# Batch 0 of a banded attention in 32 by 64 blocks, with a new order for the opening of the kernel

## The chip, the cores and the metric

One NeuronCore of a Trainium2 chip runs the whole kernel. The metric is device time in microseconds (us), the median of three runs: 878.97 us for the kernel before (878.5 to 879.45). The engines are TensorE (PE: matmul; PEld: its weight loads), VectorE (DVE), ScalarE (ACT), GpSimd (POOL) and SyncE (SP, which here only issues DMAs).

## The reference, cut to what matters

```python
# q, k, v: (8 batches, 8 heads, 576 positions, 64)
scores = q @ k.T / sqrt(64)                      # per batch and head
rel = pos[:, None] - pos[None, :]
mask_plain = (rel >= 0) & (rel < 32)                              # heads 0 to 3
mask_dil = (rel >= 0) & (rel < 128) & (rel % 4 == 0)              # heads 4 to 7
scores = where(mask, scores, -1e9); scores -= scores.max(-1)
attn = exp(scores); attn /= attn.sum(-1) + 1e-9
x = (attn @ v), heads side by side               # 4608 tokens x 512
h = x @ w_in                                     # 512 -> 2048
g = where(h >= 1, h, where(h <= -1, 0, (h + 1)**2 / 4))
return g @ w_out                                 # 2048 -> 512
```

The dilated heads become plain bands when positions are sorted by their remainder modulo 4, so every 32 queries need at most 64 keys.

## The kernel before, in words

The second half, two matrix products over 4608 tokens, is nearly all of the work. Tokens go in 9 tiles of 512; a *step* is one tile and one 128-wide slice of the 2048 hidden values: 144 steps, of which step s has tile s // 16 and slice f = s % 16. Each product is made of three fp32r products (high by high, low by high, high by low), so `layer1` (L788) of a step is 4 chunks of 3 matmuls of 128x512 and `layer2` (L861) is 4 blocks of 3. Between them stand, on ScalarE and VectorE, y = clamp(h) (L798), its square (L801), h = max(h, y) (L804), the high part of g (L815) and its low part (L819).

The weights arrive as pairs of 32-bit words and are made into high and low parts during the first 16 steps, one `wi` and one `wo` for each slice. For one of them: `scaled` (ScalarE, L218), `low_bits` (ScalarE, L224), `joined` (VectorE, L228), `high_part` (ScalarE or GpSimd, L236) and `low_part` (GpSimd, L240).

The attention of two heads (a *pair*, named by its first head n: 0, 2, 4, 6 are batch 0, 8 to 14 are batch 1) gives one of the four 128-wide chunks of x. Batch 1 is computed in blocks of 32 queries by 64 keys: 72 score matmuls for a pair (L319), ten masked minima on VectorE (L347), `exp` on ScalarE, a guard and a reciprocal, a product with the reciprocal (L407), five transposes (L434), copies to SBUF (L443), 72 value matmuls (L483), and the high and low part of x (L518, L523). Batch 0 has another path: blocks of 64 queries by 96 keys (`scores_block`, L330; minima L290), which leaves the last 64 queries of every head over; these form the *tail*, which has its own scores, softmax, transposes and values (`tail_*`, L535 to L618) between steps 2 and 4. Softmax of a pair is either *by tiles* (ScalarE subtracts the minimum and sums while it takes exp, one instruction for each tile) or *whole* (GpSimd subtracts, L373; ScalarE takes exp in one instruction, L364; VectorE sums, L377).

All that happens before step 18 is recorded from a table, `OPENING`. Each engine executes its instructions in the order in which the table's tokens stand; an engine never overtakes. A token names an operation and what it works on: `S8` scores of pair 8, `r8.3` minimum of tile 3, `z8` subtraction, `e8` exp, `u8` sum, `i8` guard, `R8` reciprocal, `n8` product with it, `T8.0` transposes, `p8.0` copy, `V8` values, `x8...` and `l8...` high and low part of x, `A2.1` chunk 1 of layer 1 of step 2, `y2 s2 j2 g2 d2` the five operations between the layers, `B2.3` block 3 of layer 2, `awi4 bwi4 jwi4 hwi4 lwi4` the five steps of a weight, `wi4`, `q8`, `k8`, `v8` loads (all on SP's queue), `W3` three filler matmuls (`spin`), `tS` to `tl` the tail. From step 18 on, the rest (`burst`, L767, and `plan`) follows fixed rules that the change does not touch; the first burst is in step 18 and needs the PSUM banks that batch 1 used. `PLACES` says which PSUM bank a tile of the opening takes. Until they are needed for weights, the places of late weights hold batch 0's inputs (`home`).

```python
        PE.matmul(out=bank[:, :128], lhsT=half, rhs=half, start=True, stop=True)
        for token in OPENING.split():
            play(token)
```

Of the kernel before, what the change touches and what calls it, by code (L numbers as in the profile page):

```python
# [25 lines left out]
F32 = mybir.dt.float32  # L26
# [8 lines left out]
WIN, DIL = 32, 4  # L35
QT, NQ = 96, 6
# [7 lines left out]
BQ, BK, NB = 64, 96, 8  # L44
TAIL = NB * BQ
# [10 lines left out]
T5 awi1 tS0 i7 R7 l0 jwi1 q8 wi3 k8 n7 tS2 tS4 tS6 x2 p5 p4 hwi1 bwi2 lwi0 T7 V4 awo0 bwo0 lwi1 wo2 wo1 l2 tr5 tr0 p7
tr6 tr2 tr1 tr4 V6 A0.0 awi2 x4 wi4 x6 A0.1 tr7 tr3 jwo0 l4 tz A0.2 te l6 jwi2 hwo0 A0.3 A1.0 A1.1 A1.2 A1.3 S8 tu
awi3 bwi3 hwi2 y0 jwi3 s0 ti j0 g0 lwo0 lwi2 hwi3 S10 d0 r8.1 tR r8.5 r8.4 r8.9 A2.0 A2.1 A2.2 bwo1 awo1 r10.1 r10.4
y1 r10.2 r8.0 r8.2 r8.7 r10.6 r8.3 r8.6 r8.8 wo5 v8 tv wo3 q14 wi6 k14 wi7 wi5 wo10 wo9 wi9 wi8 lwi3 z8 s1 awi4 r10.7
j1 A2.3 B0.3 B0.0 B0.1 g1 d1 r10.0 jwo1 tn hwo1 lwo1 A3.0 A3.1 A3.2 tT bwo2 e8 awo2 bwi4 tp A3.3 B1.1 tV u8 y2 jwi4  # L60
wo4 s2 i8 hwi4 tx R8 r10.5 j2 n8 lwi4 y3 tl r10.3 r10.8 r10.9 bwo3 g2 bwi6 awi5 B1.0 B1.3 B0.2 B1.2 d2 jwo2 awi6 s3
bwi5 jwi5 hwo2 z10 A4.0 A4.1 A4.2 A4.3 T8.0 T8.1 lwo2 e10 p8.0 awo3 p8.1 hwi5 B2.1 B2.0 B2.2 B2.3 V8 j3 lwi5 wi10 wo8
wo11 wo7 wi13 v10 wi11 wo6 k12 bwi7 g3 bwo4 x8.1.0 jwo3 y4 d3 u10 jwi6 A5.0 A5.1 i10 hwo3 x8.0.0 x8.1.1 R10 l8.1.0
l8.0.0 lwo3 hwi6 A5.2 B3.3 A5.3 B3.0 B3.2 awo4 q12 wi12 bwi9 s4 jwo4 l8.1.1 j4 n10 hwo4 B3.1 T10.0 T10.1 g4 bwi10
p10.0 lwi6 lwo4 d4 y5 awi7 awi8 p10.1 s5 bwi8 bwo5 awo5 A6.0 B4.3 B4.2 B4.1 A6.1 A6.2 A6.3 B4.0 V10 jwi7 j5 jwi8 jwo5
# [1054 lines left out]
```

## Time and profile before

| | |
|---|---|
| median of 3 runs | 878.97 us |
| profiled execution | 878.36 us, of which the span shown in the trace is 876.5 us |
| PE busy | 866.6 us, 99% of the span |
| DVE, ACT, POOL busy | 578.2 us (66%), 368.9 us (42%), 144.8 us (17%) |
| chain that ended last | PE 94% of the span |
| granted clock of TensorE | 0.999 of full speed |

The time outside the span (1.86 us) is start and end of the execution. A busy share of 99% says that hardly any time is left in which PE has nothing to do; it does not say that all it does is useful, since the filler matmuls at the beginning count as busy too. So the profile is read for two things: when the first matmul of layer 1 can start, and what PE does or waits for after that.

### The profile page before, as it was taken

The page shows a single profiled execution, that of the slowest core. Times are in us where ns is not written, and L with a number is a line of the kernel's source. Part 1 is how long each engine was busy: PE and PEld are TensorE (multiplying, and loading weights), DVE is VectorE, ACT ScalarE, POOL GpSimd, SP SyncE. Part 2 cuts the span into 40 slices and gives each one's busy share as a digit, 9 for nine tenths or more (in the row PEclk, how much of TensorE's full clock was granted, in tenths as well). Part 3 has the DMA queues.
Part 4 walks back from the last instruction along what each step waited for, and adds up shares of the span by engine and source line. Part 5 has one row for each costly group of instructions (what it writes and reads, how often), then busy time and mean ns, then how long its engine had stood idle before and what let it go on. Part 6 is the DMA issues. An engine that isn't in the chain of part 4 may idle for free.

```text
span 876.5 us, 19402 instructions
## 1 busy us (share of the span) xinstructions
PE 866.6 (99%) x7903; PEld 713.8 (81%) x7903; DVE 578.2 (66%) x1538; ACT 368.9 (42%) x969; POOL 144.8 (17%) x147
## 2 busy tenths in 40 slices
PE   8999999999999999999999999999999999999998
PEld 7777887888888888888888888888888888888886
DVE  5866746878777777777777777777777543334333
ACT  6788744443533444344443443334434222222222
POOL 4767630111111111111110011111111000000000
PEclk9999999999999999999999999999999999999999
DMA  9993302231221112111211131101200010001001
GB/s 345 373 371 116 94 28 76 61 106 57 86 72 31 34 54 101 55 56 56 104 56 55 56 105 57 42 28 61 87 28 29 1 49 1 0 1 49 1 0 49
DMA packets 25434, 66.45 MB, mean 76 GB/s; under 512 B 2816, under 2 KB 4096, under 8 KB 25344
## 3 DMA queue, kind: packets, MB, share of 16 engines
q1 hardware_dynamic: 25056, 64.97, 21.3%
q8 instruction: 62, 1.02, 0.5%
q14 instruction: 28, 0.23, 0.1%
q10 hardware_dynamic: 288, 0.23, 0.1%
HBM read 55.75 MB, written 9.44 MB: 74 GB/s over the span
## 4 chain that ended last, share of the span: by engine, by line
PE 94%; DVE 2%; ACT 1%; DMA 1%; POOL 1%; issue 1%; DVEq 0%; SPq 0%; POOLq 0%; ACTq 0%
PE h L788 44%; PE acc L861 44%; PE att L767 4%; PE spare L767 1%; DMA wi_raw<-w_in 1%; PE o L483 0%; PE s L319 0%; DMA tc_place<-block_in 0%; DVE thirds L228 0%; ACT c_place L367 0%; POOL wo L240 0%; POOL wi L240 0%; DVE xf L712 0%; ACT gh L815 0%; PE t L434 0%
## 5 line engine op out<-in xcount | busy, mean ns | idle before, releaser
L861 PE MATMUL acc<-wo,gh 128*128 128x512 f32 x1134 | 375.2, 390 | 0.1
L788 PE MATMUL h<-xh,wi 128*128 128x512 f32 x1152 | 359.0, 393 | 0.0
L788 PEld LDWEIGHTS h<-xh,wi 128*128 128x128 f32 x1152 | 213.9, 188 | 45.5 <-DVE gl L819 0.3
L861 PEld LDWEIGHTS acc<-wo,gh 128*128 128x128 f32 x1134 | 212.8, 188 | 45.0 <-POOL wo L240 0.8
L801 ACT ACTIVATE y<-y,consts 128x512 f32<-128x512 f32 x144 | 104.2, 724 | 290.4 <-DVE y L798 290.3
L788 PE MATMUL h<-xl,wi 128*128 128x512 f32 x576 | 224.8, 390 | 0.1
L861 PE MATMUL acc<-wo,gl 128*128 128x512 f32 x567 | 221.1, 390 | 0.0
L819 DVE TENSOR_TENSOR gl<-h,gh 128x512 fp32r<-128x512 f32 x142 | 98.2, 692 | 86.4 <-ACT gh L815 85.7
L798 DVE TENSOR_SCALAR y<-h 128x512 f32<-128x512 f32 x144 | 99.4, 690 | 74.6 <-PE h L788 72.9
L804 DVE TENSOR_TENSOR h<-h,y 128x512 f32<-128x512 f32 x144 | 100.7, 699 | 67.7 <-ACT y L801 66.6
L815 ACT CAST gh<-h 128x512 fp32r<-128x512 f32 x142 | 83.3, 587 | 129.2 <-PE acc L861 79.2
L788 PEld LDWEIGHTS h<-xl,wi 128*128 128x128 f32 x576 | 108.2, 188 | 23.8 <-POOL xl L733 1.1
L861 PEld LDWEIGHTS acc<-wo,gl 128*128 128x128 f32 x567 | 106.5, 188 | 22.4 <-DVE gl L819 0.3
L696 POOL TENSOR_TENSOR c<-c 128x576 f32<-128x576 f32 x24 | 27.7, 1154 | 439.5 <-DVE c L693 439.5
L712 DVE STREAM_TRANSPOSE xf<-att 32x320 f32<-32x320 f32 x192 | 91.8, 478 | 3.9
L680 ACT ACTIVATE c<-c 128x64 f32<-128x64 f32 x216 | 72.5, 338 | 50.8 <-DVE c L667 50.8
L700 DVE STREAM_TRANSPOSE pt<-c 32x288 f32<-32x288 f32 x192 | 89.9, 468 | 3.2
L733 POOL TENSOR_TENSOR xl<-xf,xh 128x384 fp32r<-128x384 f32 (+7 forms) x48 | 41.5, 876 | 63.6 <-ACT xh L729 63.4
L680 ACT ACTIVATION_READ_ACCUMULATOR c<-c 128x1 f32 x216 | 40.7, 188 | 0.0
L667 DVE CUSTOM_DVE_ANT_0 c<-att,near 128x64 f32<-128x64 f32 x144 | 22.8, 220 | 24.6 <-PE att L767 24.6
L729 ACT CAST xh<-xf 128x384 fp32r<-128x384 f32 (+7 forms) x48 | 25.1, 575 | 1.8 <-DVE xf L712 1.8
L240 POOL TENSOR_TENSOR wo<-thirds,wo 128x512 fp32r<-128x512 f32 x16 | 22.4, 1400 | 13.8 <-ACT wo L236 13.3
(127 smaller groups left out, 453.6 us busy)
## 6 DMA issues: line engine op xcount, KB each, us to landing
thirds<-near_v_in SPq DMA_DIRECT2D x24, 576.0 KB, 4.1
out<-out SPq DMA_DIRECT2D x35, 256.0 KB, 2.8
kr<-k_in SPq DMA_DIRECT2D x28, 304.0 KB, 4.8
wi_raw<-w_in SPq DMA_DIRECT2D x16, 512.0 KB, 7.7
wo_raw<-w_in SPq DMA_DIRECT2D x16, 512.0 KB, 8.7
qr<-q_in SPq DMA_DIRECT2D x28, 288.0 KB, 5.0
vt<-v_in SPq DMA_DIRECT2D x8, 288.0 KB, 6.0
v_place<-vb_in SPq DMA_DIRECT2D x4, 512.0 KB, 8.9
```

The lines of the kernel that those rows point to most:

```text
L680: nc.scalar.activation(out=c, in_=c, func=AF.Exp, bias=self.st[:, 0, tile : tile + 1], scale=-1.0, accum_out=self.st[:, 1, tile : tile + 1],)
L700: nc.vector.transpose(out=self.pt[r : r + 32, TILES * (g // 2) : TILES * (g // 2 + 1)], in_=self.c[32 * g : 32 * g + 32, :, 32 * half : 32 ...
L712: nc.vector.transpose(out=x[r : r + 32, g % 2, :, :count], in_=values[:, :, :, 32 * half : 32 * half + 32])
L733: nc.gpsimd.tensor_tensor(out=xl, in0=x, in1=xh.bitcast(F32), op=ALU.subtract)
L767: PE.matmul(out=o, lhsT=a, rhs=b, start=True, stop=True)
L788: PE.matmul(out=hps[s], lhsT=ready[f"wi{f}"][:, w, 128 * c : 128 * c + 128], rhs=x[:, c], start=c == 0 and i == 0, stop=c == NC - 1 and i ...
L798: nc.vector.tensor_scalar(out=y, in0=hps[s], scalar1=-1.0, scalar2=1.0, op0=ALU.max, op1=ALU.min)
L801: nc.scalar.activation(out=ys[s], in_=ys[s], func=AF.Square, bias=half_t, scale=0.5)
L804: nc.vector.tensor_tensor(out=hps[s], in0=hps[s], in1=ys.pop(s), op=ALU.max)
L815: nc.scalar.copy(out=gs[s][0], in_=hps[s])
L819: nc.vector.tensor_tensor(out=gl, in0=hps.pop(s), in1=gh.bitcast(F32), op=ALU.subtract)
L861: PE.matmul(out=acc[m], lhsT=g[:, r], rhs=w[:, part], start=f == 0 and i == 0, stop=(f == NF - 1 or s == len(steps) - 2 and m == TOK // 12 ...
```

## The change

Batch 0 goes through the code of batch 1. `scores_block`, `reduce`, the tail and their inputs (`qb`, `kb`, `vb`, `vbt`, `block_in`) are gone; `q_in`, `k_in` and `v_in` now hold batch 0 too. `OPENING`, `PLACES` and `home` are new tables. Some operations may be VectorE's that were ScalarE's: `low_bits` of four weights, the guard of pairs 0 and 2, more of the copies after transposes, one high part of x. Pair 6 is normalised by VectorE as pair 4 was; other weights are cast by GpSimd. In batch 0, pair 0 is whole and pairs 2 and 6 by tiles, pair 4 whole; in batch 1, all four pairs are by tiles, where they were whole.

```diff
-BQ, BK, NB = 64, 96, 8
-TAIL = NB * BQ
...
 OPENING = """
-k2 q2 W7 k0 q0 msk Q0 K0 W6 q4 k4 wi0 k6 q6 mk1 S2.0 S0.0 S2.1 S0.1 v0 v2 wi1 v6 wi2 mk2 S0.2 S0.3 S2.3 S2.2 r0.3 r0.1
...
+W7 k0 q0 q2 mk3 k2 q4 k4 k6 q6 wi0 mk2 W2 S0 v0 wi1 wo0 v2 r0.6 r0.2 r0.4 r0.7 r0.8 r0.9 r0.5 r0.0 r0.3 r0.1 S2 S4 S6
...
-    thirds = pool.tile([128, 3 * DM], U32, tag="m", name="thirds")
-    near_vt = thirds.bitcast(F32)[:, : BLOCKS * D].rearrange("p (n m d) -> p n m d", n=2, d=D)
...
-    cast_by_pool = ('wi0', 'wo0', 'wi3', 'wo1', 'wo2', 'wi6', 'wi8', 'wo8', 'wi12', 'wi13', 'wi15', 'wi14', 'wo13', 'wo15')
+    cast_by_pool = ('wi0', 'wo0', 'wi2', 'wi3', 'wo1', 'wo2', 'wo3', 'wi8', 'wo6', 'wi12', 'wi15', 'wo13', 'wo14', 'wo15')
...
-        m = floats[w] = thirds[:, DM * (third % 3) : DM * (third % 3 + 1)]
+        m = floats[w] = third_pool.tile([128, DM], U32, tag=f"m{third % 3}", name=f"m_{w}")
...
+    low_by_vector = ('wi5', 'wo15', 'wo12', 'wi15')
+
     def low_bits(w):
+        if w in low_by_vector:
+            low = words(w)[0]
+            nc.vector.tensor_scalar(out=low, in0=low, scalar1=29, scalar2=None, op0=ALU.logical_shift_right)
+            return
...
-    kept_by_vector = {1, (12, 0), 3, 7}
+    kept_by_vector = {(0, 0), (2, 0), (2, 1), (4, 0), (6, 0), (6, 1), (8, 0), (10, 0), (12, 0), (14, 0), (14, 1)}
...
+    x_by_vector = {(10, 1, 1)}
...
-    copied_by_vector = (2,)
+    copied_by_vector = (2, 3)
...
         elif token == "mk3":
-            nc.sync.dma_start(out=near, in_=near_in.rearrange("p (k j) -> p k j", k=6))
+            nc.scalar.dma_start(out=near, in_=near_in.rearrange("p (k j) -> p k j", k=6))
...
+    value_pool = ctx.enter_context(tc.tile_pool(name="value", bufs=1))
+    near_vt = value_pool.tile([128, 2, BLOCKS // 2, D], F32, name="near_vt")
```

How the order moves, on three engines. First PE around the end of layer 1 of step 1 before: `h_1` is the PSUM tile of step 1, `s_0` and `s_1` the score banks of pair 8, a matmul of 128x512 is layer 1, one of 32x64 a score block.

```order
L788 MATMUL h_1_505<-xh_366,wi_420 128x512 x2
L788 MATMUL h_1_505<-xl_367,wi_420 128x512
L319 MATMUL s_0_519<-kr_404,qr_400 32x64 x2
L319 MATMUL s_1_520<-kr_404,qr_400 32x64 x4
L319 MATMUL s_0_519<-kr_404,qr_400 32x64 x4
```

And the same place in the changed kernel: `acc_0` is the output tile of layer 2, `h_2` the tile of step 2.

```order
L574 MATMUL h_1_646<-xh_439,wi_581 128x512 x2
L574 MATMUL h_1_646<-xl_440,wi_581 128x512
L650 MATMUL acc_0_689<-wo_639,gh_683 128x512
L650 MATMUL acc_0_689<-wo_639,gl_684 128x512
L650 MATMUL acc_0_689<-wo_639,gh_683 128x512
L574 MATMUL h_2_693<-xh_439,wi_641 128x512 x2
L574 MATMUL h_2_693<-xl_440,wi_641 128x512
```

Before, the scores of pairs 8 and 10 stand behind step 1 and then step 2 follows; now a block of layer 2 of step 0 stands there at once, and the scores of pairs 8 and 10 come later, among steps 3, 0 and 1.

VectorE of the changed kernel ahead of the first low parts of x that pairs 4 and 6 give: `m_wi`, `m_wo` are weights in the making (`joined`), `xl` a low part of x, `pts` the copy of transposes, `c_place` a pair's softmax.

```order
L320 TENSOR_TENSOR c_place<-c_place,stats 128x576
L190 SCALAR_TENSOR_TENSOR m_wi_459<-m_wi_459,wi_raw 128x512
L404 TENSOR_TENSOR xl_440<-o_0_468,xh_439 128x288
L340 COPY pts_xl<-t_0_532 128x512
L340 COPY pts_xl<-t_1_537 128x128
L404 TENSOR_TENSOR xl_440<-o_1_469,xh_439 128x224
L190 SCALAR_TENSOR_TENSOR m_wo_579<-m_wo_579,wo_raw 128x512
L190 SCALAR_TENSOR_TENSOR m_wi_585<-m_wi_585,wi_raw 128x512
L404 TENSOR_TENSOR xl_440<-o_0_539,xh_439 128x2x128
L404 TENSOR_TENSOR xl_440<-o_1_540,xh_439 128x2x128
```

The stretch that stood there before, between the low part of pair 0 and that of pair 4 (L523 is the low part, L550 the tail's minima; each minimum has a second row, for its result):

```order
L523 TENSOR_TENSOR xl_367<-o_346,xh_366 128x512
L550 ISA tc_place<-tsb,tc_place 64x96
L550 ISA tc_place 64x1
L550 ISA tc_place<-tsa,tc_place 64x96
L550 ISA tc_place 64x1
L439 COPY pts_xl<-t_424 96x512
```

Eight minima of the tail have gone from VectorE's list there; the normalisation of pair 6, copies and smaller low parts have come.

ScalarE ahead of the high part of weight wi4, before (`wi_750` in the first fence, `wi_898` in the second): `c_518` and `c_729` are the softmax of pair 8.

```order
L364 ACTIVATE c_518<-c_518 128x576
L218 ACTIVATE thirds<-wo_raw 128x512
L224 ACTIVATE wi_raw<-wi_raw 128x512
L588 COPY pt_68<-tt 96x512
L801 ACTIVATE y_743<-y_743,consts 128x512
L392 ACTIVATE stats<-stats 128x9
L236 CAST wi_750<-thirds 128x512
```

and now:

```order
L587 ACTIVATE y_769<-y_769,consts 128x512
L399 CAST xh_445<-o_1_591 128x2x16
L174 ACTIVATE m_wi_776<-wi_raw 128x512
L186 ACTIVATE wi_raw<-wi_raw 128x512
L284 ACTIVATE c_729,stats<-c_729,stats 128x64 x9
L308 ACTIVATE stats<-stats 128x9
L198 CAST wi_898<-m_wi_717 128x512
```

One exp of 128x576 has become nine of 128x64, each with a sum, and they stand right ahead of the cast of wi4.

## Rows read from the trace of the kernel before

**Rows 1.** Waits of PE from 26 to 150 us: total, times, longest.

```profile
PE att L767 <- DVE xl L523: 1.1, 1, 1.1
```

**Rows 2.** Timeline of PE: start us, us, line, tiles, count, idle before and releaser.

```profile
0.92 5.17 PE L265 MATMUL h<-consts 128*128 128x128 f32 x26 [0.92 <-DVE consts L979]
...
12.95 0.61 PE L429 MATMUL t<-tc_place,c 128*96 128x128 f32 x4 [1.11 <-DMA tc_place<-block_in]
...
15.30 1.28 PE L265 MATMUL h<-consts 128*128 128x128 f32 x10
...
26.28 0.73 PE L788 MATMUL h<-xh,wi 128*128 128x512 f32 x2
...
28.46 0.63 PE L788 MATMUL h<-xh,wi 128*128 128x512 f32 x2
...
31.99 1.73 PE L319 MATMUL s<-kr,qr 64*32 64x64 f32 x144
33.66 0.73 PE L788 MATMUL h<-xh,wi 128*128 128x512 f32 x2
...
40.60 0.60 PE L584 MATMUL tt<-tc_place 128*96 128x128 f32 x4
...
42.52 0.45 PE L598 MATMUL to<-pt,tv_place 96*64 96x64 f32 x8
...
43.39 0.50 PE L861 MATMUL acc<-wo,gh 128*128 128x512 f32 x1
...
46.26 0.62 PE L788 MATMUL h<-xh,wi 128*128 128x512 f32 x2
...
48.99 0.71 PE L434 MATMUL t<-ident,c 128*128 128x128 f32 x5
...
52.49 1.25 PE L483 MATMUL o<-pt,vt 64*64 64x32 f32 x72
```

**Rows 3.** The load issued second (1.1 to 1.2 us): size, us to landing.

```profile
q_place<-qb_in SPq DMA_DIRECT2D x1, 288.0 KB, 3.6
```

**Rows 4.** Timeline of DVE, columns as in rows 2.

```profile
7.29 0.26 DVE L290 CUSTOM_DVE_ANT_0 c<-s,tc_place 128x96 f32<-128x96 f32 x1 [6.42 <-PE s L330]
...
19.22 0.55 DVE L407 TENSOR_TENSOR c_place<-c_place,sums 128x384 f32<-128x384 f32 x1
...
22.17 1.22 DVE L228 SCALAR_TENSOR_TENSOR thirds<-thirds,wi_raw 128x512 uint32<-128x512 uint32 x1
...
26.55 0.69 DVE L228 SCALAR_TENSOR_TENSOR thirds<-thirds,wo_raw 128x512 uint32<-128x512 uint32 x1
...
32.37 0.69 DVE L819 TENSOR_TENSOR gl<-h,gh 128x512 fp32r<-128x512 f32 x1 [0.65 <-ACT gh L815]
...
35.21 0.22 DVE L347 CUSTOM_DVE_ANT_0 c<-s,near 128x64 f32<-128x64 f32 x1
...
35.35 0.22 DVE L347 CUSTOM_DVE_ANT_0 c<-s,near 128x64 f32<-128x64 f32 x1
...
38.77 0.74 DVE L377 TENSOR_REDUCE stats<-c 128x9 f32<-128x576 f32 x1
```

**Rows 5.** Timeline of POOL, columns as in rows 2.

```profile
22.80 2.97 POOL L240 TENSOR_TENSOR wi<-thirds,wi 128x512 fp32r<-128x512 f32 x2
...
36.15 1.15 POOL L373 TENSOR_TENSOR c<-c,stats 128x576 f32<-128x576 f32 x1 [2.21 <-DVE stats L347]
...
42.86 0.29 POOL L406 TENSOR_TENSOR c<-c,stats 128x64 f32<-128x64 f32 x1 [1.91 <-DVE stats L398]
43.23 1.15 POOL L407 TENSOR_TENSOR c<-c,stats 128x576 f32<-128x576 f32 x1
44.34 1.29 POOL L240 TENSOR_TENSOR wi<-thirds,wi 128x512 fp32r<-128x512 f32 x1
```

**Rows 6.** Timeline of ACT, columns as in rows 2.

```profile
37.85 0.67 ACT L364 ACTIVATE c<-c 128x576 f32<-128x576 f32 x1
...
156.54 0.33 ACT L680 ACTIVATE c<-c 128x64 f32<-128x64 f32 x1
```

More of the change, by code (lines that the diff above doesn't have):

```diff
@@ L56 @@
[L56 to L65, printed above, removed]
@@ new lines @@
+x4.0.0 x4.1.0 l2.1.0 jwo0 jwi2 l4.0.0 l4.1.0 x6.1.0 bwi3 x6.0.0 lwi1 hwo0 hwi2 A0.1 A1.0 A0.2 lwo0 lwi2 awi3 l6.1.0
+l6.0.0 A0.3 A1.1 A1.2 y0 A1.3 jwi3 x6.0.1 x4.0.1 bwo1 x4.1.1 s0 hwi3 j0 lwi3 g0 y1 d0 B0.0 A2.0 s1 awo1 A2.1 A2.2
+l6.0.1 l4.0.1 l2.1.1 j1 jwo1 A2.3 g1 awi4 hwo1 d1 A3.0 A3.1 S8 lwo1 y2 awo2 bwo2 s2 x6.1.1 awi5 bwi4 wi6 wo3 v8 wo8
+wo6 wi7 wi9 k12 wo7 wo10 wo15 wo4 wo5 wi8 wo9 jwo2 r8.8 l6.1.1 r8.5 r8.1 r8.9 r8.6 r8.0 r8.7 r8.3 r8.2 j2 r8.4 B1.0
+A3.2 B0.1 B1.1 S10 B0.3 A3.3 B1.3 e8.7 e8.0 e8.2 e8.8 e8.5 e8.3 e8.4 e8.6 e8.1 jwi4 bwi5 i8 hwi4 g2 r10.9 r10.6 r10.0
@@ L319, in scores @@
             PE.matmul(out=out, lhsT=q0, rhs=k0, start=True, stop=True)
-    def scores_block(n, t):
-        if n not in scored:
-            for j in range(2):
-                scored[n + j] = bank(f"s{n + j}")
-        for half in range(2):
-            first = 2 * BQ * t + BQ * half if n < H // 2 else (CLS + 32) * t + BQ * half
-            for j in range(2):
-                r = slice(64 * j, 64 * j + 64)
-                PE.matmul(
-                    out=scored[n + j][BQ * half : BQ * (half + 1), BK * t : BK * (t + 1)],
-                    lhsT=whole["q", n][r, BQ * (2 * t + half) : BQ * (2 * t + half + 1)],
-                    rhs=whole["k", n][r, first : first + BK],
-                    start=True,
-                    stop=True,
-                )
     def lowest(n, t):
-        if n < H:
-            kind = 0 if t == 0 or n >= H // 2 else 1
-            return reduce(n, t, (scored[n][:, BK * t : BK * (t + 1)], bmsk()[:, kind]))
         j, slot = divmod(t, 4) if t < 8 else (t - 8, 4)
@@ L492, in pieces @@
         if h < H // 2:
-            first = part * 3 * QT
-            cuts = sorted({first, min(max(end, first), first + 3 * QT), first + 3 * QT})
+            first = part * HALF
+            cuts = sorted({first, min(max(end, first), first + HALF), first + HALF})
             for a, z in zip(cuts, cuts[1:]):
@@ L509, in pieces, with x_high @@
         return out
[L511 to L521 removed]
+    x_by_vector = {(10, 1, 1)}
+    def x_high(n, part, piece):
+        src, t, place = pieces(n, part)[piece]
+        copy = nc.vector.tensor_copy if (n, part, piece) in x_by_vector else nc.scalar.copy
+        copy(out=place(xtile(t)[0][:, n % H // 2]), in_=src)
@@ L522, in x_low @@
+    def x_low(n, part, piece):
+        src, t, place = pieces(n, part)[piece]
         xh, xl = (x[:, n % H // 2] for x in xtile(t))
         nc.vector.tensor_tensor(out=place(xl), in0=src, in1=place(xh).bitcast(F32), op=ALU.subtract)
-    def tail_scores(n):
-        if "s" not in tail:
-            tail["s"] = [bank("tsa"), bank("tsb")]
-        at = BK * (n // 2)
-        for j in range(2):
-            r = slice(64 * j, 64 * j + 64)
-            q0, k0 = whole["q", n][r, TAIL:], whole["k", n][r]
-            o = tail["s"][j][:, at : at + BK]
-            if n < H // 2:
-                PE.matmul(out=o[r], lhsT=q0, rhs=k0[:, TAIL : TAIL + BK], start=True, stop=True)
-                continue
-            k0 = k0.rearrange("p (c i) -> p c i", c=DIL)[:, :, 128:]
-            for w in range(2):
-                PE.matmul(
-                    out=o[64 * j + 32 * w : 64 * j + 32 * w + 32].rearrange("p (c i) -> p c i", c=2),
-                    lhsT=q0[:, 32 * w : 32 * w + 32],
-                    rhs=k0[:, 2 * w : 2 * w + 2],
-                    start=True,
-                    stop=True,
-                )
@@ L1067 @@
-    vbt = np.stack(vbt, axis=1).reshape(BK, 12 * D)
-    row, col = np.arange(128)[:, None], np.arange(BK)[None, :]
-    at = row % BQ
-    normal = (col > at) & (col <= at + WIN)
-    begins = normal & ((row >= BQ) | (col >= 32))
-    last = (col // 48 == at // 16 % 2) & (col % 48 > at % 16) & (col % 48 <= at % 16 + WIN)
-    block = [np.where(m, 0.0, NEG).astype(np.float32) for m in (begins, normal, last)]
-    block = np.concatenate([*block, np.eye(128, dtype=np.float32)], axis=1)
-    def filled(a):
-        return np.concatenate([a, np.zeros((128 - a.shape[0], a.shape[1]), a.dtype)])
```

332 lines of the change are left out of this document (74 added, 258 removed), and 10 rows, old and new, of the table PLACES.

## The prediction

> **What bounds the kernel now.** I read three views in this order: the waits of PE, PE's timeline over the opening, and then the timelines of the engines that feed it there. The waits show that once layer 1 of step 0 has begun, PE stands still once: 1.1 us before the first burst in step 18, for a low part of x [rows 1]. So the span of 876.5 us is 26.28 us until that beginning, and a stream of matmuls behind it with almost no hole [rows 2]. Three things can change the time: when the stream starts, how much PE work stands in it, and what waits are in it. That other engines are busier or idler counts only where it moves one of these. The opening is a chain through all engines: PE runs fillers until the scores, VectorE takes minima from 7.29 us on [rows 4], and the first transposes wait 1.1 us for the identity's load [rows 2]. The profiled execution took 878.36 us, 0.61 below the median of 878.97; I work in differences and take them off the median.
>
> I compare the two kernels at one point, the first matmul of step 2. Before it is at 33.66 us [rows 2].
>
> **The start of the scores.** Nine fillers stand ahead instead of 13. The 13 took 5.17 us as 26 matmuls, 0.40 each [rows 2], so nine end at 4.5. Now k0 and q0 are loaded first. The second load landed 3.6 us after its issue at about 1.16, so at 4.8 [rows 3]; the mask beside it is twice as large, so I take 5.0. One pair's scores are half of 1.73 [rows 2], with the pipeline's filling 1.0, so VectorE can begin at 6.1 instead of 7.29 [rows 4].
>
> **From the minima to the values.** A minimum of 128x64 follows the one before it in 0.14 to 0.15 [rows 4], so ten end at 7.6. Pair 0 is done whole: subtraction 1.15 on GpSimd [rows 5] to 8.9, exp 0.67 on ScalarE [rows 6] behind two tiles of pair 2, to 9.6, sum 0.74 on VectorE [rows 4] behind other minima to 10.4, guard and reciprocal to 10.8, product 0.29 and 1.15 on GpSimd [rows 5] to 12.4. The identity is now behind 192 + 4 x (304 + 288) + 512 KB of loads, 3.1 MB with itself, as before with its smaller pieces; it let the transposes start at 12.95 [rows 2], and I take 12.8. So the first transposes gain almost nothing: the 1.2 us of the earlier start go into a softmax that is half as wide again on GpSimd and VectorE.
>
> Then PE's list is bound by what it holds: transposes of pair 2 behind GpSimd's next product at 14.1, values of pair 0 (1.25 to 1.3, [rows 2]) to 15.8, eight fillers of 0.256 (1.28 for five, [rows 2]) to 17.9. Pair 4's transposes wait for its product on VectorE: 0.55 for 384 columns [rows 4] makes 0.83 for 576, with 0.25 for the extra tile, behind a `joined` and a sum, so 18.7. Pair 2's values then run to 20.5, where layer 1 of step 0 begins, against 26.28. But its chunk 0 needs pair 0 alone; transposes of pair 6 (0.5), two value products (1.3 each) and three chunks (0.69 each) follow, and chunk 3 could start at 25.8 by PE.
>
> VectorE has more to do until then. From the product of pair 4 it still has three low parts, a copy of 0.6, pair 6's product (1.1), two more copies, three `joined`, two low parts of pair 2 and four of pairs 4 and 6: 7.5 us, if each `joined` takes 0.69 [rows 4], which ends at 26.2. Beside a busy GpSimd one took 1.22 [rows 4, 5]; by the two rows each of the products and `joined` costs 0 to 0.53 more. I take 0.7 in all, so chunk 3 starts at 26.9. In the trace, from that chunk of step 0 (28.46) to the end of the low part of g (33.06) it is 4.6 us [rows 2, 4], through five operations that each need the one before; VectorE was late once by 0.2, so I take 4.5. Before, the scores of pairs 8 and 10 filled that stretch; now PE has only step 1 to put there and then stands about 1.6 us until 31.4, a new wait. Behind it are one block of layer 2 (0.69) and then step 2, at 32.1: 1.6 us earlier than before.
>
> **What has been done by then, and what not.** One block of layer 2 is ahead: -0.7. The scores of pairs 8 and 10 are still to come: 1.73 before [rows 2], 2.0 apart, since each change of the matmul's shape costs a refill. The tail never comes: from 40.60 its transposes take 0.35 of PE, and its values 0.87 from 42.52 to 43.39 [rows 2], with refills 1.4. Together -0.7 + 2.0 - 1.4 = -0.1.
>
> **The burst.** The 1.1 us wait [rows 1] was for low parts of pair 14 that stood last in VectorE's list, behind step 17. They now stand ahead of step 16. What is late next is the low part of g of step 17, whose bank the burst also takes; it ends within 0.1 of the burst. I take -1.0.
>
> **Other edits.** Four `low_bits` on VectorE: the trace of before shows no such instruction; by the nearest rows it is between 0.22 (a minimum) and 1.22 (a `joined` beside GpSimd) [rows 4]. I take 0.69, the `joined` alone, the nearest in form: 2.8 us in all, hidden since steps 5 and 12 to 15 have no wait of PE. Without that cover it would be at most 4.9. Copies, guards and the cast moved between engines are of the same kind: some tenths each, beside layer 1 and 2. That `near_vt` has its own place changes no wait of PE. SP's queue: q8 no longer waits for the tail's scores; instead k12 waits for pair 8's scores, with wo7, wo10, wo15, wo4 and wo5 behind it. They land some 8 us later than that wait ends, still ahead of step 4's layer 2. In batch 1, exp by tiles puts nine of 0.33 [rows 6] in place of one of 0.67 on ScalarE: +2.3 for each of pairs 8 and 10, while a subtraction of 1.15 goes from GpSimd and a sum of 0.74 from VectorE. The cast of wi4 is behind the first nine. Its low part ended at 45.63 [rows 5] and step 4 began at 46.26 [rows 2], 0.6 later. I walked ScalarE's list with these durations and found wi4 ready at 44.9 where step 4 could begin at 44.6. I put 0.3 for this.
>
> **Sum.** -1.6 - 0.1 - 1.0 + 0.3 = -2.4. Forecast: 878.97 - 2.4 = 876.6 us, itself good to about 1 us either way.
>
> **Rivals.**
>
> *The gain is lost on VectorE.* The chain to chunk 3 of step 0 is VectorE's list without a hole. If the two products and the `joined` there all run beside GpSimd, four more at 0.53 are 2.1 instead of 0.7, and a late start of the minima adds 0.3: 1.7 more. That gives 878.3, no change that can be told. For it: GpSimd is at work in most of the stretch from 22 to 26 us [rows 5]. Against: the low parts and the copies, half of the list, read PSUM. The Trainium skill speaks for this rival: "GPSIMD Engine Reference", section "Key points", says that GpSimd shares its SBUF interfaces with VectorE, with contention for VectorE instructions that have two SBUF inputs. The two `joined` rows agree with it (0.69 alone, 1.22 beside GpSimd), and so by that rule moving pair 6's product to VectorE is dear.
>
> *ScalarE makes the weights late.* The 18 tile exps stand in order ahead of casts that PE needs. If both runs push the weights back in full, 4.6 us of waits stand before steps 4 and 5 and layer 2 of step 3 in place of my 0.3: 876.6 + 4.3 = 880.9, slower than before. It decides from the point where waits behind step 2 exceed 2.7 us, that is if wi4's low part ends after 47.3 us. For it: wi4 had only 0.6 us to spare. Against: GpSimd, which makes the low part, loses the subtraction there, and ScalarE the tail's exp, copy and cast.
>
> *More is gained.* If the loads are faster now that they are not cut in halves, and VectorE meets GpSimd seldom, step 2 comes at 31.0 and no weight waits: 876.6 - 1.1 - 0.3 = 875.2.
>
> **How the numbers follow.** The forecast case has 0.50 (its own range 875.6 to 877.6), the loss on VectorE 0.23, late weights 0.11, more gain 0.16. A difference of 0.2%, 1.76 us, is about what a measurement here can tell from none: faster is below 877.2, slower above 880.7. Faster: all of the third case, some 0.37 of the forecast's 0.50 and 0.04 of the first rival, 0.57. Slower: 0.10. Same: 0.33. The range takes in the first rival with its own spread and most of the better case, and reaches up halfway into the case of late weights: 874.6 to 879.8.
>
> **What would show it.** Right: minima from about 6.1 us, first transposes near 12.8, layer 1 of step 0 near 20.5, a wait of PE of some 1.6 us for the low part of g of step 0, step 2 near 32.1, no wait before the burst. The first rival is right if step 2 comes after 33.3 and VectorE has no idle time from 15 to 27 us; the second if PE waits for GpSimd's low parts of wi4 or wo3 by more than 1 us each. I am wrong in kind if the identity or k0 holds up the opening beyond 14 us, or if PE's granted clock falls in the stretch with the new wait; in the opening before it was full throughout, with idle pieces of 1.1 us and more.

## The result and the profile after

The changed kernel takes 888.75 us (median of four runs, 887.91 to 889.23) beside 878.96 for the kernel before: 1.0109 times as long, 95% interval 1.0096 to 1.0122. The forecast was 876.6, so even the sign was wrong. The profiled execution has a span of 887.1 us against 876.5.

Most of the loss lies ahead of 45 us. The waits of PE over the whole span of the changed kernel (total, times, longest):

```profile
PE o L366 <- issue: 3.7, 2, 3.5
PE s L256 <- issue: 3.6, 1, 3.6
...
PE acc L650 <- ACT gh L604: 0.9, 1, 0.9
...
PE acc L650 <- DVE gl L608: 0.2, 1, 0.2
```

The last two are the forecast's new wait ahead of layer 2 of step 0 (1.1 in place of 1.6). The wait before the burst [rows 1] is gone. New, and in no rival, are the first two: 7.3 us of "issue", in which PE waited for nothing that the profile names. PE's timeline of the changed kernel shows where they stand (L256 scores, L226 fillers, L335 transposes, L366 values, L574 layer 1, L650 layer 2; x is the number of matmul records):

```profile
0.92 4.21 PE L226 MATMUL h<-consts 128*128 128x128 f32 x18 [0.92 <-DVE consts L761]
5.22 1.08 PE L256 MATMUL s<-kr,qr 64*32 64x64 f32 x72
7.47 0.96 PE L256 MATMUL s<-k_place,q_place 64*32 64x64 f32 x72 [1.16 <-DMA k_place<-k_in]
9.00 1.12 PE L256 MATMUL s<-k_place,q_place 64*32 64x64 f32 x59 [0.57 <-DVE stats L264]
13.71 1.57 PE L256 MATMUL s<-k_place,q_place 64*32 64x64 f32 x85 [3.59 <-issue]
15.21 2.93 PE L226 MATMUL h<-consts 128*128 128x128 f32 x12
17.93 1.27 PE L335 MATMUL t<-ident,c 128*128 128x128 f32 x5
...
25.44 0.89 PE L366 MATMUL o<-pt,v_place 64*64 64x32 f32 x47
26.56 0.59 PE L366 MATMUL o<-pt,v_place 64*64 64x32 f32 x25 [0.23 <-issue]
27.08 0.73 PE L574 MATMUL h<-xh,wi 128*128 128x512 f32 x2
...
29.59 0.52 PE L366 MATMUL o<-pts_xl,v_place 64*64 64x32 f32 x21
33.60 1.70 PE L366 MATMUL o<-pts_xl,v_place 64*64 64x32 f32 x51 [3.49 <-issue]
35.24 1.22 PE L574 MATMUL h<-xh,wi 128*128 128x512 f32 x2
...
39.24 0.86 PE L574 MATMUL h<-xh,wi 128*128 128x512 f32 x2
...
44.59 0.63 PE L574 MATMUL h<-xh,wi 128*128 128x512 f32 x2
```

Both long stops fall inside a pair's products, after the 59th of 72 records and after the 21st, where no new operand begins. The first transposes come at 17.93, layer 1 of step 0 at 27.08, its chunk 3 at 39.24 and step 2 at 44.59, where the kernel before had 12.95, 26.28, 28.46 and 33.66 [rows 2]. By step 2 the loss is 10.9 us; behind it 0.3 come back, which leaves the 10.6 between the spans.

Adding up the x column, with every row, PE stops after records 221, 474 (0.23 us) and 600. The distances are 253 and 126, and each record has a weight load beside it: 126 are some 252 instructions. The DMA queue 8, of kind "instruction", carries 64 packets with 1.05 MB, 16.4 KB each; PE has 8159 matmuls and 8159 weight loads in the whole run, 255 for each packet. The DMA view of the changed kernel shows, for 11.1 to 11.2 and for 31.1 to 31.2 us, one of them starting (packets, MB, share of 16 engines over the 0.1 us, so each took about 1.1 us):

```profile
q8 instruction: 1, 0.02, 66.7%
...
q8 instruction: 1, 0.02, 68.4%
```

They end near 12.2 and 32.3; PE goes on 1.5 and 1.3 us later. Up to 40 us the queue's packets start at 11.1, 17.4, 24.0, 31.1 and 37.2, each some 3.5 to 4.5 us after PE passes record 95, 221, 347, 474 or 600, steps of 126 or 127. My reading: PE ran out of code. The Trainium skill bears on it ("Runtime: NRT & Kernel Launch", section "Instruction fetch mechanics"): code comes in blocks of 16 KiB, 256 instructions, and the crossing is mostly hidden. The trace agrees on the block, and shows a case where it isn't hidden.

The second loss is the granted clock. Windows of the changed kernel (PE, PEld, DVE, ACT, POOL busy with counts, PE clock, DMA share, GB/s): the time around 9.0 us, the first stop, from it to the transposes, the second stop, and from it on.

```profile
8.00:10.00 2.00, 1.43 (x97) 1.19 (x86) 1.64 (x21) 1.34 (x5) 1.15 (x1) 0.76 1.04 402
...
10.10:13.70 3.60, 0.02 (x2) 0.00 (x0) 0.04 (x2) 2.36 (x14) 0.00 (x0) 0.50 1.03 394
13.70:17.90 4.20, 4.19 (x97) 4.02 (x97) 3.56 (x28) 0.44 (x2) 1.44 (x2) 0.50 1.05 402
...
30.10:33.60 3.50, 0.01 (x2) 0.00 (x0) 2.30 (x4) 1.10 (x3) 2.89 (x5) 0.90 1.03 397
33.60:39.90 6.30, 6.29 (x62) 5.26 (x62) 1.26 (x2) 2.98 (x8) 1.22 (x1) 0.51 0.97 380
```

At 0.50 (1.2 of 2.4 GHz) three chunks of layer 1 take 4.0 us (35.24 to 39.24), against 2.2 before [rows 2]; the 12 filler records at 15.21 take 2.93, where ten took 1.28 [rows 2]. That the first stop brought the first fall is not shown: the clock is at 0.51 from 9.0 to 10.1 us already, ahead of the stop and behind PE's waits of 1.16 us for pair 2's k and 0.57 us for a bank. The loads run at some 400 GB/s throughout: the code comes through DMA engines that are full.

### The profile page after: what moved, and what is told of

Same layout as the page of the kernel before. It is cut to its first block, busy times and chain, and to the rows that moved or that the text cites. A ratio compares the mean times of both kernels' runs of the same rounds, so it can differ in the third digit from the quotient of the medians.

```text
span 887.1 us, 19968 instructions
## 1 busy us (share of the span) xinstructions
PE 870.1 (98%) x8159; PEld 716.4 (81%) x8159; DVE 581.6 (66%) x1544; ACT 372.7 (42%) x1038; POOL 132.4 (15%) x136
## 3 DMA queue, kind: packets, MB, share of 16 engines
q8 instruction: 64, 1.05, 0.5%
## 4 chain that ended last, share of the span: by engine, by line
PE 94%; DVE 2%; ACT 1%; issue 1%; DMA 1%; POOL 0%; SPq 0%; DVEq 0%; ACTq 0%; POOLq 0%
PE h L574 44%; PE acc L650 43%; PE att L553 4%; PE o L366 1%; PE spare L553 1%; PE s L256 1%; PE t L335 1%; DMA k_place<-k_in 1%; PE h L226 0%; DVE y L584 0%; ACT y L587 0%; ACT c L284 0%; ACT gh L604 0%; DVE h L590 0%; DVE xf L498 0%
## 5 line engine op out<-in xcount | busy, mean ns | idle before, releaser
L650 PE MATMUL acc<-wo,gh 128*128 128x512 f32 x1134 | 376.2, 390 | 0.9 <-ACT gh L604 0.9
L574 PE MATMUL h<-xh,wi 128*128 128x512 f32 x1152 | 360.6, 394 | 0.0
L574 PEld LDWEIGHTS h<-xh,wi 128*128 128x128 f32 x1152 | 214.6, 189 | 45.6
L650 PEld LDWEIGHTS acc<-wo,gh 128*128 128x128 f32 x1134 | 212.8, 188 | 46.5 <-POOL wi L198 1.3
L574 PE MATMUL h<-xl,wi 128*128 128x512 f32 x576 | 225.3, 391 | 0.1
L650 PE MATMUL acc<-wo,gl 128*128 128x512 f32 x567 | 221.0, 390 | 0.2 <-DVE gl L608 0.2
L574 PEld LDWEIGHTS h<-xl,wi 128*128 128x128 f32 x576 | 108.6, 189 | 23.9 <-POOL xl L519 0.8
L650 PEld LDWEIGHTS acc<-wo,gl 128*128 128x128 f32 x567 | 106.5, 188 | 22.8 <-DVE gl L608 0.8
L553 PE MATMUL att<-near_vt,pt 64*32 64x64 f32 x1728 | 24.2, 226 | 0.0
```

Source lines behind the costliest of these rows:

```text
L553: PE.matmul(out=o, lhsT=a, rhs=b, start=True, stop=True)
L574: PE.matmul(out=hps[s], lhsT=ready[f"wi{f}"][:, w, 128 * c : 128 * c + 128], rhs=x[:, c], start=c == 0 and i == 0, stop=c == NC - 1 and i ...
L650: PE.matmul(out=acc[m], lhsT=g[:, r], rhs=w[:, part], start=f == 0 and i == 0, stop=(f == NF - 1 or s == len(steps) - 2 and m == TOK // 12 ...
```

## The experiments

The theory: PE's place in the program is bound by its code in the opening. The rivals: a wait for data that the trace doesn't name; VectorE or GpSimd as the real bound.

**A count moved.** Edit on the changed kernel's list:

```diff
-... S2 S4 S6 W6 r2.1
+... W6 S2 S4 S6 r2.1
```

> The changed kernel with six fillers (12 matmul records) moved from behind the scores of pair 6 to ahead of those of pair 2; nothing else moves. Theory (TensorE's code comes in blocks of 16 KB on queue 8, and PE runs out of code): the first stall stands at a count of instructions, so it moves from the 59th record of pair 4's scores to the 47th; the second stays at the 21st record of pair 6's second value product, since the count ahead of it is the same. The block is asked for when PE passes record 95, some 0.7 us earlier than before, so the stall ends at about 13.0 us instead of 13.7, and the time is 0.5 to 1.5 us below the changed kernel's 888.75. Rival (a wait for data that the trace doesn't name, a load of q or k): the stall stays at the 59th record, which needs the data that it needed before, and the time is unchanged.

PE's timeline of this run around the two stops:

```profile
9.08 0.70 PE L256 MATMUL s<-k_place,q_place 64*32 64x64 f32 x47 [0.34 <-DVE stats L264]
13.49 1.77 PE L256 MATMUL s<-k_place,q_place 64*32 64x64 f32 x97 [3.71 <-issue]
...
29.91 0.52 PE L366 MATMUL o<-pts_xl,v_place 64*64 64x32 f32 x21
32.64 1.56 PE L366 MATMUL o<-pts_xl,v_place 64*64 64x32 f32 x51 [2.21 <-issue]
```

The stop went from the 59th record to the 47th and the second stayed at the 21st: a wait for data would have stayed at the 59th. Both are again the 221st and the 600th record of PE. 887.31 us (885.1 to 888.41), as expected but for the end of the first stop, 13.49 where I had 13.0.

**Fewer records in the same time.** Fillers up to 512 columns wide:

```diff
-        for _ in range(times):
-            PE.matmul(out=bank[:, :128], lhsT=half, rhs=half, start=True, stop=True)
+        while times:
+            wide = min(times, 4)
+            rhs = half_t.broadcast_to([128, 128 * wide])
+            PE.matmul(out=bank[:, : 128 * wide], lhsT=half, rhs=rhs, start=True, stop=True)
+            times -= wide
```

> The changed kernel with fillers of up to 512 columns in place of up to four of 128 each: the same PE time in 34 records fewer, 12 of them ahead of the first stall. Theory (PE's code): the first stall moves from the 59th record of pair 4's scores to the 71st, the second from the 21st record of pair 6's second value product to the 55th; the time falls by 0.3 to 1.5 us, since PE does that much more ahead of each stall. Rival (a data wait): the stalls stay at their records.

PE's timeline of this run, the rows at the stops:

```profile
8.74 0.93 PE L259 MATMUL s<-k_place,q_place 64*32 64x64 f32 x71 [0.60 <-DVE stats L267]
13.12 1.46 PE L259 MATMUL s<-k_place,q_place 64*32 64x64 f32 x73 [3.45 <-issue]
...
28.85 0.99 PE L369 MATMUL o<-pts_xl,v_place 64*64 64x32 f32 x55
33.76 0.66 PE L369 MATMUL o<-pts_xl,v_place 64*64 64x32 f32 x17 [3.92 <-issue]
```

71 and 55, to the record. The time stays at 888.72 (886.24 to 889.18), where I expected 0.3 to 1.5 us less: 34 records are worth no time that can be told while the blocks come no sooner.

**Only code added, to the kernel before.** Seven fillers become 70 small products; each of either shows as two records, so there are 126 more:

```diff
+        if times in (2, 3):
+            few = half_t[:64].broadcast_to([64, 32])
+            for i in range(10 * times):
+                out = bank[32 * (i % 4) : 32 * (i % 4 + 1), 32 * (i // 4) : 32 * (i // 4 + 1)]
+                PE.matmul(out=out, lhsT=few, rhs=few, start=True, stop=True)
+            return
```

> The kernel before, with its seven fillers behind pair 0's first transposes (14 matmul records of 128 columns, 1.8 us) replaced by 140 records of 32 rows by 32 columns that take about as long: 126 records, some 252 instructions more, about one code block, and no other edit. Theory (PE's code): the boundary that the kernel before passes at about 25 us is passed some 7 us earlier, before its block has landed; PE stands 2 to 3.5 us inside pair 0's values or the transposes behind them with no releaser shown, layer 1 of step 0 begins at 28 to 29.5 instead of 26.3, and the time is 880 to 882.5. Rival (instructions cost only their own time): layer 1 begins within 0.5 us of 26.3 and the time is within 0.5 us of the kernel before.

PE's timeline of this run:

```profile
15.35 1.05 PE L267 MATMUL h<-consts 64*32 64x32 f32 x100
...
17.34 0.92 PE L474 MATMUL o<-pts_xh,v_place 96*64 96x64 f32 x24
21.30 2.40 PE L474 MATMUL o<-pts_xh,v_place 96*64 96x64 f32 x40 [3.04 <-issue]
...
30.11 0.72 PE L794 MATMUL h<-xh,wi 128*128 128x512 f32 x2
```

The last 100 small records take 1.05 us, where ten of a filler took 1.28 [rows 2], and yet PE stops 3.04 us in pair 0's values, after record 346, and layer 1 begins at 30.1, later than I expected. 882.78 us beside 879.33, 1.0039 times (1.0023 to 1.0054); I had expected at most 882.5. A block of code is enough to make the kernel before slower, with no other part of the change.

**Loads in smaller pieces.** SyncE keeps eight loads in flight, so smaller ones should leave less ahead of the code. Weights in halves or quarters of partitions (v in halves), then weights in halves of columns; last, columns with both filler edits. The edit for halves (the others cut in the same way):

```diff
-        nc.sync.dma_start(out=raw, in_=source[w[:2]][:, int(w[2:])].bitcast(U32))
+        for p in (0, 64):
+            half = slice(p, p + 64)
+            nc.sync.dma_start(out=raw[half], in_=source[w[:2]][half, int(w[2:])].bitcast(U32))
```

> The changed kernel with every load of a weight and of a batch-0 or batch-1 v cut in two halves of 64 partitions. SyncE keeps eight loads in flight, so about half as many bytes stand ahead of a block of TensorE's code. Theory (code comes late because it queues behind the loads): a code block starts about 2 us after PE passes the boundary instead of 3.5 to 4.6, both stalls of 3.6 and 3.5 us shrink to 2 us or less each, and the time falls to 881 to 885 us. Rival (a data wait): the same bytes land in the same order at about the same times, both stalls stay at 3.5 us within 0.4, and the time is 888 to 890.

> As the one with halves, but every weight in quarters of 32 partitions (v in halves). Theory (code queues behind loads): the code's delay shrinks further, to 1 to 1.5 us, the stalls to 1.5 us or less, the clock of PE stays at its high level from the first layer 1 on, and the time is 877 to 883 us; against it works that SyncE's issues at 0.33 us each for 128 KB nearly bound the loads. Rival (a data wait): stalls of 3.5 us as before or longer.

> The changed kernel with every weight loaded in two halves of columns (all 128 partitions, 2 KB each). In the two runs with loads of 64 and 32 partitions the loads moved only some 250 GB/s instead of 400, so that data became late; here the rate should stay near 400. Theory (code queues behind the loads issued before it): some 2.2 MB in flight instead of 3.2, a code block starts 2 to 3 us after PE passes its boundary instead of 3.5 to 4.6, each of the two stalls is about 1 us shorter, and the time is 884 to 887.5. Rival (the delay of the code doesn't depend on the loads ahead of it): stalls of 3.6 and 3.5 as before and 888 to 890.

> The changed kernel with three edits: weights in halves of columns, the six fillers ahead of pair 2's scores, and fillers of up to 512 columns in place of four of 128 (34 matmul records fewer ahead of the second stall, in the same PE time). Theory (PE is bound by its code from 8 to 34 us): each record fewer brings the stalls later in the program, each microsecond less of delay comes off twice, and the time is 881 to 885.5. Rival (code isn't the bound): no better than 887.

All four missed what I expected: 899.55 (892.65 to 903.99), 905.85 (903.26 to 907.0), 887.42 (884.08 to 888.0) and 887.5 us (885.24 to 889.31). The DMA view from 14 to 30 us, of the changed kernel and, in the second fence, of the one with halves of partitions:

```profile
DMA packets 2339, 6.38 MB, mean 398 GB/s; under 512 B 258, under 2 KB 258, under 8 KB 2335
```

```profile
DMA packets 1626, 3.94 MB, mean 246 GB/s; under 512 B 324, under 2 KB 324, under 8 KB 1621
```

With loads to 64 partitions two fifths of the rate were gone (quarters: 214 GB/s), and weights came late: PE waited 8.2 and 10.0 us for GpSimd's high part of a `wo`. The first stop stood at the 59th record and was longer, 4.7 us in both, but with loads this slow that says little of the code. With columns, which halve the size of a load too, the rate held (387 GB/s), but the stops were 3.3 and 3.7 us, about as without the edit (with the filler edits 3.9 and 2.4), and the theory's sentence on bytes in flight isn't shown by it.

**Loads held back.** The bytes ahead of a block were then taken away in another way. q of pair 2 is put in the place of wi0, so that SyncE, in order, holds wi0 and all behind it until PE has read that q:

```diff
-"q2": "wi8", ...
+"q2": "wi0", ...
```

> The changed kernel, where q of pair 2 borrows the place of wi0 instead of wi8, so that SyncE holds wi0's load, and all loads behind it, until PE has done pair 2's scores (about 8.4 us instead of 4.85). Theory (a code block queues behind the loads that were issued before it): at about 7.5 us, when PE passes record 95, only some 0.3 MB are ahead instead of 1.5, so the block starts at 8.3 to 9 us instead of 11.12 and PE's first stall is 0.5 to 1.5 us instead of 3.6; the later blocks meet a full queue again, so the second stall stays at 2 to 4 us; the time is 883 to 886.5. Rival (code is late for another reason than the loads ahead): the first block starts at 10.5 to 11.5 as in all runs of the changed kernel so far, the first stall stays over 3 us, and with the loads held the time is 888 to 891.

PE's timeline of this run, the rows at the stops:

```profile
9.12 0.80 PE L256 MATMUL s<-k_place,q_place 64*32 64x64 f32 x59 [0.63 <-DVE stats L264]
11.36 1.57 PE L256 MATMUL s<-k_place,q_place 64*32 64x64 f32 x85 [1.44 <-issue]
...
18.97 1.12 PE L366 MATMUL o<-pt,v 64*64 64x32 f32 x59 [0.41 <-issue]
...
25.29 0.59 PE L366 MATMUL o<-pt,v_place 64*64 64x32 f32 x25 [1.10 <-issue]
...
31.84 1.70 PE L366 MATMUL o<-pts_xl,v_place 64*64 64x32 f32 x51 [3.01 <-issue]
```

The first block starts at 9.0 us instead of 11.1, by the DMA view of 9 to 10 us, which has one packet of queue 8 at 181 GB/s in all; the stop is 1.44 instead of 3.59, at the same record. Between the two kernels only the held loads differ, so loads issued ahead do delay the code. The 0.41 us at 18.97 stand after record 346, the boundary between 221 and 474 that cost the changed kernel nothing. The time, 887.44 (887.06 to 887.93), is above what I expected: the stops at the later boundaries (0.41, 1.10, 3.01) are 0.8 us longer together than the later ones of the changed kernel. All stops together are 6.0 us instead of 7.3, and the time is 1.3 us lower.

With two more holds (q of pair 6 in the place of wo0, v of head 2 in that of wo2), and then with six fillers moved as well:

> As the one that holds wi0, and besides q of pair 6 in the place of wo0 and v of head 2 in that of wo2: SyncE holds wo0 until pair 6's scores and wo2 until pair 2's values are done. Theory (code behind loads): each of the blocks that PE wants in the opening finds little ahead of it, no stall without a releaser is longer than 1.5 us, the granted clock stays high from layer 1 of step 0 on, chunk 3 of step 0 begins at 28 to 31 us instead of 39.2, and the time is 877.5 to 882. Rival (the three pairs' softmax and VectorE bound the opening anyway): the stalls go but waits for VectorE or GpSimd take their place, and the time stays over 884.

> As the one that holds three loads, with six fillers moved ahead of pair 2's scores. Theory: PE passes record 95 some 0.7 us earlier while the queue is a little fuller, and the first transposes lose a filler ahead of them, so within 0.7 us of the one without the move. If the granted clock, which fell at 9.0 us in the changed kernel after the waits for pair 2's k and pair 4's bank, falls later or not at all here, up to 2 us less.

Three holds: 887.03 (884.11 to 887.1), stops of 2.2 and 2.9 us, where I expected none over 1.5. With the fillers moved: 881.99 us, 5.0 less, where I expected 2 at most. Its executions lie in two groups, six at 881.6 to 882.4 and three at 885.8 to 886.6; the profiled one is of the lower, without a second stop. There the block behind record 474 starts to come at 26.6 us, about 1.1 us after PE passes that record; with three holds alone it starts at 29.5, 4.1 us after. The holds are the same, and no run shows why. Its PE and, in the second fence, its VectorE timeline:

```profile
12.23 1.23 PE L256 MATMUL s<-k_place,q_place 64*32 64x64 f32 x97 [2.27 <-issue]
16.20 1.33 PE L335 MATMUL t<-ident,c 128*128 128x128 f32 x5 [2.75 <-POOL c L320]
...
28.50 1.67 PE L366 MATMUL o<-pts_xl,v_place 64*64 64x32 f32 x72
```

```profile
12.71 0.23 DVE L264 CUSTOM_DVE_ANT_0 c_place<-s,near 128x64 f32<-128x64 f32 x1 [2.05 <-PE s L256]
...
12.86 0.75 DVE L294 TENSOR_REDUCE stats<-c 128x9 f32<-128x576 f32 x1
```

The sum of pair 0 (12.86) stands behind a minimum of pair 4 (12.71), whose scores PE had no code for. So a stop in pair 4 makes pair 0's transposes late. The next two runs put that sum, with guard, reciprocal and product, ahead; the first has wide fillers too:

```diff
-... r4.3 u0 r4.9 i0 r4.6 R0 r4.1 n0 e2.5
+... u0 i0 R0 n0 r4.3 r4.9 r4.6 r4.1 e2.5
```

> As the one with three holds and the fillers ahead of pair 2's scores (881.7 us, first stall 2.3, first transposes at 16.2 behind a wait of 2.7 for GpSimd's product), with two more edits: fillers of up to 512 columns (22 matmul records fewer ahead of the first stall), and in the lists of VectorE and GpSimd the sum, guard, reciprocal and product of pair 0 ahead of the first minima of pair 4. Theory: the wait of 2.7 us is the stall passed on, since VectorE stands at a minimum of pair 4, whose scores PE hasn't the code for, with pair 0's sum behind it; so with the sum ahead the first transposes come at 13.3 to 14.2 us, layer 1 of step 0 at 23 to 24.5 and its chunk 3 at 29 to 31 us (32.3 without these edits), and the time is 878 to 880.5. Rival (pair 0's product is late by its own chain, or the transposes wait for the identity): the transposes stay after 15.5 us and the time at 881 or more.

> As the one with three holds and six fillers moved (881.99), with one more edit: sum, guard, reciprocal and product of pair 0 ahead of the first minima of pair 4; the fillers stay 128 columns wide, so that all instruction counts are those of that run. It tells two things apart that the run with all edits mixed. Theory: a stall's place is set by the count of instructions and its length by how soon PE passes 126 more records; with the old count the boundary that cost 3.0 us there (54 records later, between two value products) falls where it cost nothing before, so no second stall over 1 us; the first transposes come at 13.3 to 14.2, chunk 3 of step 0 at 29.5 to 31.5, and the time is 878.5 to 881. Rival (the sum ahead of the minima is what made the second stall, by bringing PE to the boundary before its block): a stall of 2 to 3.5 us in pair 4's or 6's value products again, and 883 to 886.

PE's timelines, first with all edits, then without the wide fillers:

```profile
13.34 0.74 PE L338 MATMUL t<-ident,c 128*128 128x128 f32 x5 [0.15 <-DMA ident<-ident_in]
...
25.77 0.99 PE L369 MATMUL o<-pts_xl,v_place 64*64 64x32 f32 x55
29.79 0.44 PE L369 MATMUL o<-pts_xl,v_place 64*64 64x32 f32 x17 [3.02 <-issue]
```

```profile
13.68 1.33 PE L335 MATMUL t<-ident,c 128*128 128x128 f32 x5
...
31.22 1.70 PE L366 MATMUL o<-pts_xl,v_place 64*64 64x32 f32 x51 [2.89 <-issue]
```

The transposes came at 13.3 and 13.7, so the passing-on through VectorE's list is shown. The totals missed: 885.16 (883.7 to 885.72) and 883.76 (881.22 to 886.32, again in two groups, three at 881.2 to 882.3 and three at 885.2 to 886.3). PE reaches the boundary inside the last value product sooner (26.8 and 28.3 us, against 29.0 with the fillers moved) and stands there 3 us again, at the record that its count says (55 and 21). My thought that this boundary "cost nothing before" came from one profile of the lower group; this last profile, with the stop, is of the upper. That the second stop makes the two groups is likely, but two profiles of two kernels don't show it. Group by group the last run is no faster than the one before the sum was moved, so the earlier transposes are worth nothing that can be told here.

**The burst alone.** On the kernel before, x14.1.1, l14.1.1 and l14.0.1 made in steps 14 to 16:

```diff
-... x14.1.0 x14.0.1 x14.0.0 d14 ... l14.1.0 l14.0.0 A16.3 ... g16 x14.1.1 d16 ... od3 l14.1.1 l14.0.1 od0 od2
+... x14.1.0 x14.0.1 x14.0.0 x14.1.1 d14 ... l14.1.0 l14.0.0 l14.1.1 l14.0.1 A16.3 ... g16 d16 ... od3 od0 od2
```

> The kernel before with one part of the change alone: the last high part and the last two low parts of pair 14's attention output are made in step 14 to 16 instead of behind step 17. Theory (the prediction's term for the burst): the 1.1 us wait of PE ahead of the first burst goes and nothing else moves, 1.0 us less than the kernel before: 877.9. Rival (something else, the low part of g of step 17, is as late): within 0.3 us of before.

877.49 us (median of 11) beside 878.61 (15), 0.9992 times, interval 0.9983 to 1.0001; the span is 875.7 against 876.5 and PE has no wait longer than 0.2 us from 26 to 150. It is the only version here below both kernels, by 1.1 us in the medians, though the interval just takes in no change.

## Why the prediction was wrong, point by point

- **The step that failed** is "From the minima to the values", with its "PE's list is bound by what it holds". I let PE run its list as fast as operands come and never asked whether its code was there. The stops (3.59, 0.23, 3.49) are 7.3 us, beside the 12.5 by which step 2 missed the forecast's 32.1.
- **The clock.** Most of the rest is work at 1.2 GHz: pair 4's and 6's scores and the fillers up to 17.9, then the values and first chunks after 33.6. By the rows above, 12 filler records took 2.93 where ten took 1.28 [rows 2], 51 value records 1.70 where 72 take 1.25, and three chunks 4.0 instead of 2.2; some 4 us together, an estimate from these rows. I had named a falling clock for the stretch with the new wait, where it stayed at 1.00, and held the opening to be safe; there it fell, and I had priced nothing for it. What made it fall the first time is open: in the changed kernel it fell at 9.0 us, and with three holds at 7.5, ahead of the first stop; in the run with all edits the first stop of 2.46 us brought no fall (1.00 up to 31 us).
- **The start** was right: minima at 6.3 us (forecast 6.1), scores at 5.2 (5.0). The nine fillers ended at 5.13, not 4.5, which by luck cost nothing: where they ended earlier (4.7 us, with three holds), the scores waited for q until 5.1. The first transposes came at 17.9 instead of 12.8; with the sum ahead and the stop cut to 2.5 and 2.3 us they came at 13.3 and 13.7, so most of this miss comes from the stop.
- **From chunk 3 of step 0 to step 2** the forecast had 5.2 us, with the new wait; it took 5.35 (39.24 to 44.59). This term held.
- **First rival (VectorE).** Wrong as the cause: VectorE stood idle 4.1 us for pair 4's scores at the first stop and 3.6 for a high part of x behind the second. Its sign nearly came out all the same: step 2 came after 33.3, and VectorE was idle only 0.9 us from 15 to 27, with its list pushed there by the stop. Its price was met now and then, as VectorE's timeline of the changed kernel shows: a product of 64 columns took 0.92 while GpSimd made a low part (22.48 to 23.75) and 0.22 without, and one `joined` took 1.11 beside a low part (28.91 to 30.19). And I had misread a row: the `joined` of 0.69 that the prediction calls alone, at 26.55 in the trace of before [rows 4], ran beside GpSimd as well (26.60 to 27.93), as the second fence shows, from GpSimd's timeline of before; the next `joined` there, at 28.48, took 0.68 while GpSimd made a low part (from 28.56). In both places it was GpSimd's operation that was long: 1.33 us where one of the same size took 0.83 (at 22.02), and 1.76 where a low part of the changed kernel took 1.27. So the two `joined` rows do not show what they were quoted for. In all these places the operation that started second was the long one; but a low part of g at 43.27 in the changed kernel took 0.68 beside GpSimd's low part from 42.42 on, so it is no rule that the runs show.

```profile
22.91 0.92 DVE L319 TENSOR_TENSOR c_place<-c_place,stats 128x64 f32<-128x64 f32 x1
...
26.28 0.22 DVE L319 TENSOR_TENSOR c_place<-c_place,stats 128x64 f32<-128x64 f32 x1
...
29.62 1.11 DVE L190 SCALAR_TENSOR_TENSOR m_wo<-m_wo,wo_raw 128x512 uint32<-128x512 uint32 x1
```

```profile
26.60 1.33 POOL L563 TENSOR_TENSOR tc_place<-tc_place 128x384 f32<-128x384 f32 x1 [0.83 <-DVE tc_place L550]
```

- **Second rival (late weights).** Did not happen: from 45 to 200 us PE waits 1.0 us in all, none of it for a weight. My 0.3 for wi4 isn't there either; with all else 11 us later it could not be tested.
- **Behind step 2** the forecast had -0.1 - 1.0 + 0.3 = -0.8; the spans give -0.3. The burst's wait is gone in both runs, and the medians of the run alone differ by 1.1, near the forecast's 1.0, though not clear of noise; the other 0.5 I have not broken down.

What stays open: how much of a block's delay hangs on bytes in flight. The hold shows that loads ahead of it matter, the halves of columns did not shorten it. And no run of the new opening was free of stops, so whether it would then come to the forecast is not shown. The run with all edits speaks against it: its first transposes were near the forecast, yet layer 1 of step 0 began at 23.2 instead of 20.5, behind waits of 1.55 us for GpSimd's product of pair 2 and 1.21 for VectorE's of pair 4.

The trace of before had a sign of it. It has 364 matmul records ahead of layer 1 of step 0 and 367 ahead of its chunk 1, where the changed kernel's list has 499 and 651; those 284 more are over two blocks of code. And queue 8's packets of before start at 11.8, 21.0, 29.1 and 36.1 us, some 2.3 to 3.4 us after PE passes records 95, 221, 347 and 474: each block already took that long to begin, but there PE needed over 7 us from one boundary to the next.

## What to carry to other kernels

Count TensorE's instructions in a dense stretch of small products. Where 126 matmuls with their weight loads pass in less time than a block of code takes to come (6 to 7 us from one boundary to the next here while loads filled the DMA engines), PE stops with "issue" as releaser, in the middle of a group; spreading such products between long ones is what I would try next (no run here did), and holding loads that aren't needed yet shortened the first stop here, though not yet the time of the kernel by itself. A stop can also make other engines late through their lists, as it did the first transposes, and the work behind it slow, where the granted clock falls.

## What the runs showed of the hardware that was not expected

- A stop for code ended 1.3 to 1.5 us after its packet had landed (12.2 to 13.7, 32.3 to 33.6), and PE went on at 13.7, 26.6 and 33.6, two blocks and one block apart: 6.4 and 7.0 us for each.
- The stops stood after PE's record 221, 346, 474 or 600 in every run whose stops are given here, the one of the kernel before with 126 records more among them.
- The granted clock fell to 1.2 GHz in every run with a long stop and stayed there while PE was again fully busy (4.19 of 4.20 us at 0.50); but it fell ahead of the first stop in two of them, and one stop of 2.46 us brought no fall.
- With weights loaded to 64 and 32 partitions at a time the DMA moved 246 and 214 GB/s from 14 to 30 us, where loads to 128 moved 398, and 387 when cut by columns.
- A VectorE product of 64 columns took 0.92 us beside GpSimd and 0.22 without (changed kernel); a `joined` of 512 columns took 1.22 where GpSimd's operation had started first (22.02 against 22.17), and 0.69 where it started second (26.60 against 26.55) and itself took 1.33 instead of 0.83 (kernel before).
